# Float64 conversion through a PSUM bank, the last tile's values product in column halves, and another order of the start

## The chip, the cores and the metric

The kernel runs on one core of a Trainium2 chip. The metric is the device time of one execution in microseconds (us), lower is better; it was timed three times, and a further execution was recorded by the hardware profiler.

## The reference

Inputs are q, k and v of 4 batches, 8 heads, 576 positions and 64 columns in float32, and weights in float64: `w_in` 512x2048, `w_out` 2048x512, and for the second MLP `w_gate` and `w_val` 512x1536, `w_out` 1536x512 and a vector `rms_g`. Attention is causal by blocks of 64 positions; its 2304 rows of 512 pass a mish MLP, an RMS norm and a gated MLP:

```python
scores = scale * np.matmul(q, k.transpose(0, 1, 3, 2))
scores = np.where(block_i >= block_j, scores, -1000000000.0)
attn = np.exp(scores - np.max(scores, axis=-1, keepdims=True))
attn = attn / (np.sum(attn, axis=-1, keepdims=True) + 1e-09)
x = np.matmul(attn, v)                      # then (2304, 512)
h = x @ w_in
x = (h * np.tanh(softplus(h))) @ w_out
xn = x / np.sqrt(np.mean(x * x, axis=-1, keepdims=True) + 1e-06) * rms_g
g = xn @ w_gate
out = (g / (1 + np.exp(-g)) * (xn @ w_val)) @ w_out
```

## The kernel before

**Stages.** Attention goes batch by batch, in tiles of 128 queries; 576 queries make four whole tiles and a last one of 64. Such a tile holds scores (`scores`, L986 in f32, L991 and L992 in f16 with the mask), exponentials and their transposes (`probs`), the values product (`av`, L1155 and L1163) and the division by the row sums (`norm_x`, L1195, tile `xfl`). The first MLP has nine tiles of 256 tokens and eight steps of 256 hidden columns in each: the product `h` (L1377 for the first tile, L1386 for the others), the mish function, and the product `y` (L1455 for the first tile, L1447 for the others). The second MLP follows, with `mlp2_o` at its end. Where a product is f16, each factor is split into a high and a low half, and three products are summed (`PASSES`). Scores and values products of batch 0's first tiles, and the whole first MLP tile, are f32.

**The last tile.** Its 64 queries of two heads stand side by side in the 128 columns of one weight tile. The scores go to the two halves of the partitions in matmuls of 64 weight columns (L1009 in f16, L1002 in f32). The values product takes all 128 columns as weights and the 128 value columns of both heads as the moving side (L1163), so half of what it makes is not read: `norm_x` takes the two wanted squares of 64 in two operations.

**Weights.** A float64 chunk (128x512 numbers, 512 KB) is loaded into one of four raw buffers (`load64`, L574, tile `wir` for `w_in`, `wor` for `w_out`, `w2rg`, `w2rv`, `w2ro` for the second MLP in half chunks). Three operations of VectorE build float32 out of the two words of each number (`to_f32`): L586 shifts the high word's mantissa and exponent into place, L594 brings the sign, L614 adds the low word's bits. All three write the destination in SBUF (`wis`, `wos`), the second and third read it again. Column sums (`wiq`, L630), a scale, and the split into f16 halves follow.

**PSUM.** All eight banks are taken: two for `h`, two for `s`, one for `x` (the values product; third bank of `mlp2_o`), two for `y`, and one, `shared`, half of which is `c` (small column sums, L499, L1647; read by VectorE at L501 and L1652), while idle products write into the other half.

**Order.** Each piece of work is recorded by `op(...)` with engine, cost, readers and writers into a `Plan`. A list scheduler (`place`) gives each a planned start from costs and due times, moved by tables (`SHIFT` by part, `FINE` by operation; `PICK` chooses an engine), and the program is emitted in that order. In planned gaps of TensorE in the first 60 us `with_idle` puts idle 128x128 products. The program begins with the queries and all key tiles of batch 0, then the values and `w_in`; attention tiles 0 and 1 come ahead of the first MLP tile, and tile 2 is placed by due time. SyncE issues all loads from one queue, in order.

## Time and profile before

| | us |
|---|---|
| timed runs: lowest, median, highest | 947.88, 949.21, 949.57 |
| profiled execution | 945.24 |
| its span in the trace | 943.5 |
| granted clock of TensorE, mean | 1.00 |

The span is what lies between the first and the last recorded instruction; the profiled execution's own time lies 1.7 us above it, and 4.0 us below the median of the timed runs. TensorE (PE) does the matrix products, VectorE (DVE) the conversions, maxima and normalisations, ScalarE (ACT) the exponentials, GpSimd (POOL) further elementwise work, and SyncE (SP) issues the loads.

### The profile page before, as it was taken

How to read it: one execution, taken by the hardware profiler on the slowest of the kernel's cores; microseconds unless marked ns; L12 is line 12 of the kernel's file. 1: busy time of each engine (PE TensorE's matmuls, PEld its weight loads, DVE VectorE, ACT ScalarE, POOL GpSimd, SP SyncE). 2: the span in 40 equal slices, each digit the busy share in tenths (PEclk: the TensorE clock that was granted, in tenths of full speed). 3: DMA queues.
4: the chain of work that ended last, by engine and by line, in shares of the span. 5: the costliest groups of instructions: out<-in, count | busy, mean ns of one | idle time of the engine just before them, and what ended most of it. 6: DMA issues, size and time to landing. Idle time of an engine off the chain costs nothing. (4 is left out here: it accounts for less than half of the span.)

```text
span 943.5 us, 19993 instructions
## 1 busy us (share of the span) xinstructions
PE 916.3 (97%) x7221; PEld 630.7 (67%) x7221; DVE 816.2 (87%) x1913; ACT 644.4 (68%) x1341; POOL 520.0 (55%) x642
## 2 busy tenths in 40 slices
PE   8999999999999999999999999999999999999997
PEld 7786467476676756667575855767676776767676
DVE  4899989998795868899875999989999999997776
ACT  4669769999797998878674657657666465553431
POOL 1259156484672447557612828589757579573421
PEclk9999999999999999999999999999999999999999
DMA  9864696799757696687863767736295470717011
GB/s 218 215 216 129 195 177 121 130 162 180 152 121 134 111 182 123 141 164 165 171 137 45 125 200 152 140 96 118 79 196 103 121 122 15 140 28 153 6 68 68
DMA packets 317187, 125.44 MB, mean 133 GB/s; under 512 B 296352, under 2 KB 296352, under 8 KB 317088
## 3 DMA queue, kind: packets, MB, share of 16 engines
q1 hardware_dynamic: 317088, 124.17, 62.4%
q8 instruction: 56, 0.92, 0.4%
q14 instruction: 43, 0.35, 0.1%
HBM read 50.07 MB, written 12.98 MB: 67 GB/s over the span
## 5 line engine op out<-in xcount | busy, mean ns | idle before, releaser
L1386 PE MATMUL h<-x,w1i 128*128 128x256 f16 x1536 | 180.5, 273 | 2.1 <-ACT f L1412 1.8
L1447 PE MATMUL y<-w1o,g 128*128 128x512 f16 x768 | 178.9, 379 | 2.0 <-DVE w1o L559 1.6
L1386 PEld LDWEIGHTS <-w1i 128*128 128x128 f16 x1536 | 146.4, 98 | 25.4 <-issue 4.4
L1994 PE MATMUL o<-w2o,pp 128*128 128x256 f16 x1134 | 137.7, 273 | 1.6 <-DVE pp L1904 1.1
L1994 PEld LDWEIGHTS <-pp 128*128 128x128 f16 x1134 | 110.6, 98 | 23.9 <-DVE pp L1904 1.6
L1447 PEld LDWEIGHTS <-g 128*128 128x128 f16 x768 | 71.3, 98 | 80.7 <-issue 4.4
L1835 PEld LDWEIGHTS <-w2g 128*128 128x128 f16 x756 | 73.9, 98 | 47.5 <-issue 2.9
L1835 PEld LDWEIGHTS <-w2v 128*128 128x128 f16 x756 | 73.9, 98 | 46.6 <-issue 2.2
L1051 ACT ACTIVATE e<-s,bias,cS 128x512 f32<-128x512 f32 (+4 forms) x120 | 72.5, 607 | 20.8 <-POOL bias L1035 10.8
L1835 PE MATMUL v_u<-xnT,w2v 128*128 128x384 f16 x432 | 81.6, 326 | 0.3 <-DVE c5v L1916 0.2
L1835 PE MATMUL g_u<-xnT,w2g 128*128 128x384 f16 x432 | 80.1, 326 | 0.4 <-DVE sl11g L1916 0.3
L1026 DVE TENSOR_REDUCE mx<-s 128x1 f32<-128x512 f32 (+4 forms) x128 | 69.9, 556 | 7.1 <-PE s L992 5.9
L1132 POOL TENSOR_TENSOR p<-e,p 128x128 f16<-128x128 f32 (+4 forms) x60 | 56.6, 946 | 33.1 <-ACT p L1128 21.2
L1429 DVE SCALAR_TENSOR_TENSOR g<-f,ich,g 128x512 f16<-128x512 f32 x64 | 54.6, 857 | 10.4 <-ACT g L1424 9.3
L1163 PEld LDWEIGHTS <-pt 128*128 128x128 f16 x1128 | 48.6, 98 | 21.9 <-DMA pt<-p 8.3
L1835 PE MATMUL g<-xnT,w2g 128*128 128x384 f16 x324 | 61.1, 326 | 0.9 <-DVE sl12g L1916 0.6
L1835 PE MATMUL v<-xnT,w2v 128*128 128x384 f16 x324 | 61.5, 326 | 0.5 <-DVE u2v L1916 0.3
L1163 PE MATMUL x<-v,pt 128*128 128x64 f16 (+1 forms) x1128 | 55.0, 199 | 6.4 <-DMA pt<-p 4.9
L1051 ACT ACT_TABLE_LOAD x40 | 51.3, 1283 | 3.5 <-DVE p L1132 2.5
L1412 ACT ACT_TABLE_LOAD x40 | 51.3, 1283 | 2.3 <-PE h L1386 0.9
L1412 ACT ACTIVATE f<-h,ch 128x512 f32<-128x512 f32 x64 | 43.4, 685 | 11.4 <-PE h L1386 6.9
L1035 POOL TENSOR_SCALAR bias<-mx,nS 128x1 f32<-128x1 f32 (+1 forms) x49 | 24.3, 497 | 29.7 <-DVE mx L1026 16.7
(350 smaller groups left out, 2107.9 us busy)
## 6 DMA issues: line engine op xcount, KB each, us to landing
wir<-in_moe_w_in_dram SPq DMA_DIRECT2D x16, 512.0 KB, 5.4
wor<-in_moe_w_out_dram SPq DMA_DIRECT2D x16, 512.0 KB, 4.3
w2rg<-in_moe_w_gate_dram SPq DMA_DIRECT2D x24, 256.0 KB, 3.3
w2rv<-in_moe_w_val_dram SPq DMA_DIRECT2D x24, 256.0 KB, 3.2
w2ro<-in_moe_w_out_dram SPq DMA_DIRECT2D x24, 256.0 KB, 2.9
q<-in_q_dram SPq DMA_DIRECT2D x16, 256.0 KB, 3.7
k<-in_k_dram SPq DMA_DIRECT2D x16, 256.0 KB, 4.2
v<-in_v_dram SPq DMA_DIRECT2D x15, 256.0 KB, 3.8
```

Of the source, the lines that this page charges most:

```text
L1026: lambda z=z, cols=cols: nc.vector.reduce_max(out=mx()[:, cols], in_=ts[z](), axis=AX.X),
L1035: bias_of = lambda eng: eng.tensor_scalar(out=bias()[:, key : keys[-1] + 1 : 2], in0=mx()[:, 2 * key : 2 * keys[-1] + 1 : 4], scalar1=m_op ...
L1051: lambda y=y, z=z, c0=c0, w=w, acc=acc, e=e, h=h: nc.scalar.activation(out=e()[:, c0 : c0 + w], in_=ts[z]()[:, y, :], func=AF.Exp, bias=bi ...
L1132: lo = lambda eng, z=z, ev=ev: eng.tensor_tensor(out=view(p16)[:, z, :, 1, :], in0=ev(0, kt), in1=view(p16)[:, z, :, 0, :], op=ALU.subtract)
L1163: nc.tensor.matmul(xt()[:, cols, :], pv(z)[:, t, ph, :], v16[b, t]()[:, vh, key * w : key * w + w], start=(t == 0 and y == 0), stop=(t == ...
L1386: nc.tensor.matmul(ph()[:, g, :], w1i[fq]()[:, cc, wh, f * P : (f + 1) * P], x()[:, xh * NCC + cc, :], start=(z == 0), stop=(z == 3 * NCC ...
L1412: ACT, t_act(W, 1, True), lambda: nc.scalar.activation(out=e(), in_=phf(), func=AF.Mish, scale=cs()),
L1429: lambda: nc.vector.scalar_tensor_tensor(out=g16()[:, 1], in0=hv(), scalar=sc(), in1=g16()[:, 0], op0=ALU.mult, op1=ALU.subtract),
L1447: nc.tensor.matmul(yps[t, m](), g16()[:, gh, g, m * P : (m + 1) * P], w1o[f]()[:, wh, :], start=(f == 0 and z == 0), stop=(f == NF1 - 1 an ...
L1835: nc.tensor.matmul(b(), w[wo]()[:, wh, cc, :], x()[:, (2 * xo + xh) * 2 + cc, :], start=(first and i == 0), stop=(i == 5), skip_group_chec ...
L1994: nc.tensor.matmul(b()[:, side, :], pps[r][po]()[:, gh, m * P : (m + 1) * P], w[wo]()[:, wh, r, :], start=(first and i == 0), stop=(i == 5 ...
```

## The change

- `to_f32` takes, for `w_in`, `w_out` and the first third of the gate and value weights, a new PSUM bank `v` (tile `cv`): the first two steps write there, the third reads it and writes SBUF. The rest stays as it was.
- The bank `x` is no more: the values product writes the first half of `shared` (columns 0 to 255), `c` stays in 256 to 511, and the idle products write 384 to 511. The freed bank is `v`, which is also the third bank of `mlp2_o`.
- The last tile's values product is two matmuls of 64 weight columns and 64 moving columns, one for each head, instead of one of 128 and 128; `norm_x` is one operation for all tiles.
- Batch 0's f32 keys are loaded and transposed tile by tile (`prep_k32`). Only tiles 0 and 1 of the keys and values come first; the string `START` mixes attention tile 2 and the other loads into the first MLP tile.
- Planner costs, due times and the three tables are others.

```diff
@@ -417,8 +417,13 @@
     def ps_s(shape, name):
         return psum("s", 2, shape, name)
 
-    def ps_x(shape, name):
-        return psum("x", 1, shape, name)
+    def ps_x(name):
+        b = psum("x", 1, [P, NPAIR, D], name)
+        b.whole = lambda: shared()[:, : NPAIR * D].rearrange("p (h d) -> p h d", d=D)
+        return b
+
+    def ps_v(shape, name):
+        return psum("v", 1, shape, name)
 
     def ps_y(i, shape, name):
         return psum(f"y{i}", 1, shape, name)
@@ -574,48 +579,41 @@
-    def to_f32(dst, r, at, pool=False, n=512):
+    def to_f32(dst, r, at, through=True, n=512):
...
+        if through:
+            cnt[0] += 1
+            t, t_one, t_two = ps_v([P, n], f"cv{cnt[0]}"), t_dve(n), t_dve(n)
+        else:
+            t, t_one, t_two = dst, t_dve2(n), t_dvett(n)
         op(
-            DVE, t_dve2(n),
+            DVE, t_one,
             lambda: nc.vector.tensor_scalar(
-                out=dst().bitcast(U32), in0=word(1), scalar1=0x07FFFFFF, scalar2=3,
+                out=t().bitcast(U32), in0=word(1), scalar1=0x07FFFFFF, scalar2=3,
                 op0=ALU.bitwise_and, op1=ALU.logical_shift_left,
             ),
-            r=[r], w=[dst], at=at,
+            r=[r], w=[t], at=at,
         )
         op(
-            DVE, t_dvett(n),
+            DVE, t_two,
             lambda: nc.vector.scalar_tensor_tensor(
-                out=dst().bitcast(U32), in0=word(1), scalar=0xC0000000, in1=dst().bitcast(U32),
+                out=t().bitcast(U32), in0=word(1), scalar=0xC0000000, in1=t().bitcast(U32),
                 op0=ALU.bitwise_and, op1=ALU.bitwise_or,
             ),
-            r=[r], w=[dst], at=at,
+            r=[r], w=[t], at=at,
         )
-        if pool:
-            op(
-                DVE, t_dve2(n),
-                lambda: nc.vector.tensor_single_scalar(word(0), word(0), 29, op=ALU.logical_shift_right),
-                r=[r], w=[(r, 0)], at=at,
-            )
-            op(
-                POOL, t_pool(512),
-                lambda: nc.gpsimd.tensor_tensor(out=dst().bitcast(U32), in0=dst().bitcast(U32), in1=word(0), op=ALU.add),
-                r=[(r, 0), dst], w=[dst], at=at,
-            )
-            return
         op(
-            DVE, t_dvett(n),
+            DVE, t_two,
             lambda: nc.vector.scalar_tensor_tensor(
-                out=dst().bitcast(U32), in0=word(0), scalar=29, in1=dst().bitcast(U32),
+                out=dst().bitcast(U32), in0=word(0), scalar=29, in1=t().bitcast(U32),
                 op0=ALU.logical_shift_right, op1=ALU.bitwise_or,
             ),
-            r=[r], w=[dst], at=at,
+            r=[r, t], w=[dst], at=at,
         )
 
@@ -778,15 +775,15 @@
 
     spares = buf("kv", [P, 4, 512], F32, "spares", "big1", 1)
 
+    def prep_k32(b, tt, at):
+        plan.part = f"k{b}_{tt}"
+        if b not in kT32:
+            kT32[b] = buf("at2" if b % 2 else "kv", [P, NPAIR, S], F32, f"kT32_{b}", f"kT{b % 2}", 1)
+        t = load(k, "k", b, tt, at)
+        transposed(t, f"kT32_{b}_{tt}", kT32[b], tt, at)
+
@@ -1016,10 +1013,10 @@
                 if last:
-                    op(PE, t_mm(w, 2 * passes) + 44, lambda z=z: mm_last(z), r=rd, w=[ts[z]], at=at)
+                    op(PE, t_mm(w, passes) + 60, lambda z=z: mm_last(z), r=rd, w=[ts[z]], at=at)
                 else:
                     for y in range(g):
-                        op(PE, t_mm(n, passes) + 30, lambda y=y: mm_head(y), r=rd + masks, w=[(ts[0], y)], at=at)
+                        op(PE, t_mm(n, passes) + ((100 if n == P else 190) if f32 else 30), lambda y=y: mm_head(y), r=rd + masks, w=[(ts[0], y)], at=at)
                 cols = slice(2 * key + z, 2 * keys[-1] + z + 1, 4)
@@ -1157,20 +1154,22 @@
                             start=(t == 0), stop=(t == kt - 1),
                         )
                     return
-                w = 2 * D if last else D
                 for t in range(kt):
                     for y, (vh, ph) in enumerate(PASSES):
-                        nc.tensor.matmul(
-                            xt()[:, cols, :], pv(z)[:, t, ph, :], v16[b, t]()[:, vh, key * w : key * w + w],
-                            start=(t == 0 and y == 0), stop=(t == kt - 1 and y == 2),
-                        )
+                        for hh in range(2 if last else 1):
+                            sl = slice(BLK * hh, BLK * hh + BLK) if last else slice(0, P)
+                            c0 = (2 * key + hh) * D if last else key * D
+                            nc.tensor.matmul(
+                                xt()[sl, cols, :], pv(z)[:, t, ph, sl], v16[b, t]()[:, vh, c0 : c0 + D],
+                                start=(t == 0 and y == 0), stop=(t == kt - 1 and y == 2),
+                            )
 
...
             op(
-                PE, (56 if last else 34.2) * 3 * kt, mm, r=[pt] + [v16[b, t] for t in range(kt)],
+                PE, 29.2 * 3 * kt + (150 if last else 0), mm, r=[pt] + [v16[b, t] for t in range(kt)],
                 w=[(xt, cols)], at=at,
             )
@@ -1188,16 +1187,13 @@
             xf = buf("at", [P, NPAIR, D], F32, f"xfl{b}_{i}_{half}", "xfl", 1)
-            for hh in range(2 if last else 1):
-                sl, cl = (slice(BLK * hh, BLK * hh + BLK), slice(D * hh, D * hh + D)) if last else (slice(0, P), slice(0, D))
-                op(
-                    DVE, t_dve(256, 1),
-                    lambda sl=sl, cl=cl: nc.vector.tensor_tensor(
-                        out=xf()[sl], in0=xt()[sl, :, cl], in1=r()[sl].unsqueeze(2).to_broadcast([sl.stop - sl.start, NPAIR, D]),
-                        op=ALU.mult,
-                    ),
-                    r=[xt, r], w=[(xf, hh)], at=at,
-                )
+            op(
+                DVE, t_dve(256, 1),
+                lambda: nc.vector.tensor_tensor(
+                    out=xf(), in0=xt(), in1=r().unsqueeze(2).to_broadcast([P, NPAIR, D]), op=ALU.mult,
+                ),
+                r=[xt, r], w=[xf], at=at,
+            )
             t, c0 = divmod(b * NBLK + 2 * i, BPT)
@@ -1317,12 +1313,10 @@
         return T0 + (g / BPT - LEAD) * NS1 * STEP1
 
     prep_q(0, 0, 0.0)
-    prep_k(0, 100.0, KV_PACE)
+    prep_k32(0, 0, 100.0)
+    prep_k32(0, 1, 200.0)
     prep_q(0, 1, 300.0)
-    split_k(0, 5 * KV_PACE, 100.0)
-    prep_v(0, 200.0, KV_PACE)
-    norm_v(0, 7 * KV_PACE)
-    split_v(0, 7 * KV_PACE, 100.0)
+    prep_v(0, 3500.0, 0.0, range(2))
     load_w_in(W_IN_AT, W_IN_PACE)
@@ -1562,15 +1555,28 @@
     firsts = {}
     sums_b = buf("x1", [P, 8 * HK], F32, "sums_b")
 
-    for z in range(2):
-        record_attention(z)
-    queue = [(0, s, mlp1_h(0, s)) for s in range(NS1)]
+    queue, begun = [], 2
+    for c in START:
+        kind, z = c[0], int(c[1])
+        if kind == "a":
+            record_attention(z)
+            begun = max(begun, z + 1)
+        elif kind == "h":
+            queue.append((0, z, mlp1_h(0, z)))
+        elif kind == "k":
+            prep_k32(0, z, K_AT + 1000.0 * z)
+        elif kind == "q":
+            prep_q(0, z, K_AT + 1000.0 * z)
+        elif kind == "v":
+            prep_v(0, V_AT, KV_PACE, range(2, NTT))
+            norm_v(0, VS_AT)
+            split_v(0, VS_AT, 100.0)
     split_w_in(W_SPLIT_AT, W_IN_PACE)
     load_w_out(W_OUT_AT, W_OUT_PACE)
     switch("at2", to_at2, ["rw"], W_OUT_AT)
     for z in queue:
         mlp1_y(*z)
-    order = [(att_time(*TOK[z]), 0, z) for z in range(2, len(TOK))]
+    order = [(att_time(*TOK[z]), 0, z) for z in range(begun, len(TOK))]
     order += [(t_step(n // NS1, n % NS1), 1, n) for n in range(NS1, NT1 * NS1)]
@@ -1631,7 +1637,7 @@
-                    to_f32(plan.part_of(big, cc, slice(c0, c0 + FW // 2)), r, a, n=FW // 2)
+                    to_f32(plan.part_of(big, cc, slice(c0, c0 + FW // 2)), r, a, fq == 0 and nm != "o", FW // 2)
@@ -1982,7 +1988,7 @@
                 chain["o"] += 1
                 z = chain["o"] % 3
                 name = f"o{l}_{chain['o']}"
-                banks.append(ps_y(z, [P, 2, HK], name) if z < 2 else ps_x([P, 2, HK], name))
+                banks.append(ps_y(z, [P, 2, HK], name) if z < 2 else ps_v([P, 2, HK], name))
@@ -2077,7 +2083,7 @@
-    plan.idle = lambda: nc.tensor.matmul(shared()[:, :128], ones_h(), idle_in(), start=True, stop=True)
+    plan.idle = lambda: nc.tensor.matmul(shared()[:, 384:512], ones_h(), idle_in(), start=True, stop=True)
     plan.run()
@@ -2089,206 +2095,213 @@
...
-    "": 780187, "q0_0": -295567, "k0_1": -281404, "k0_2": -105611, "k0_4": -39635, "q0_1": -632121, "v0_0": 4640,
...
-T0, STEP1 = 35000.0, 7376.0
+START = ("a0", "a1", "h0", "h1", "h2", "h3", "h4", "k2", "h5", "q2", "h6", "v0", "a2", "k3", "k4", "h7")
+K_AT, V_AT, VS_AT = 20000.0, 16000.0, 26000.0
+T0, STEP1 = 28000.0, 7376.0
 ATT0, ATT0_PACE = 5000.0, 9000.0
-W_IN_AT, W_IN_PACE = 8000.0, 700.0
-W_OUT_AT, W_OUT_PACE, W_OUT_SPLIT = 60000.0, 2472.0, 1598.0
+W_IN_AT, W_IN_PACE = 3000.0, 1000.0
+W_OUT_AT, W_OUT_PACE, W_OUT_SPLIT = 50000.0, 2472.0, 1598.0
```

SyncE's queue from the program's start, before; `q`, `k`, `v` and `spares` are tiles of batch 0's inputs, `wir` chunks of `w_in`:

```order
L758 DMA q_0_2_88<-in_q_dram 128x8x64
L758 DMA k_1_4_109<-in_k_dram 128x8x64
L758 DMA k_2_5_125<-in_k_dram 128x8x64
L758 DMA k_4_7_127<-in_k_dram 64x8x64
L758 DMA k_0_3_129<-in_k_dram 128x8x64
L758 DMA k_3_6_131<-in_k_dram 128x8x64
L574 DMA wir_0_164<-in_moe_w_in_dram 128x1024
L758 DMA q_1_8_168<-in_q_dram 128x8x64
L758 DMA spares<-in_v_dram 128x8x64
L574 DMA wir_1_192<-in_moe_w_in_dram 128x1024
L574 DMA wir_2_194<-in_moe_w_in_dram 128x1024
L574 DMA wir_3_196<-in_moe_w_in_dram 128x1024
```

and now:

```order
L755 DMA q_0_2_88<-in_q_dram 128x8x64
L755 DMA k_0_3_109<-in_k_dram 128x8x64
L755 DMA v_0_7_125<-in_v_dram 128x8x64
L579 DMA wir_0_127<-in_moe_w_in_dram 128x1024
L579 DMA wir_1_129<-in_moe_w_in_dram 128x1024
L755 DMA k_1_4_131<-in_k_dram 128x8x64
L579 DMA wir_2_164<-in_moe_w_in_dram 128x1024
L755 DMA q_1_5_168<-in_q_dram 128x8x64
L579 DMA wir_3_188<-in_moe_w_in_dram 128x1024
L755 DMA v_2_77_192<-in_v_dram 128x8x64
L755 DMA v_4_81_212<-in_v_dram 64x8x64
L755 DMA v_1_9_221<-in_v_dram 128x8x64
```

Three of the five key tiles went behind the first four chunks of `w_in`.

VectorE ahead of the first product `h`, before; L1195 normalises the second half of attention tile 1, L1026 takes row maxima of tile 2, L586, L594 and L614 convert:

```order
L614 SCALAR_TENSOR_TENSOR wis_0_685<-wir_0_354,wis_0_685 128x512
L586 TENSOR_SCALAR wis_1_730<-wir_1_456 128x512
L1026 TENSOR_REDUCE mx_735<-s_2_0_0_709 128x1
L586 TENSOR_SCALAR wis_2_744<-wir_2_470 128x512
L1026 TENSOR_REDUCE mx_735<-s_2_1_0_725 128x1
L594 SCALAR_TENSOR_TENSOR wis_2_744<-wir_2_470,wis_2_744 128x512
L1187 RECIPROCAL r_766<-r_82_728 128x4
L594 SCALAR_TENSOR_TENSOR wis_1_730<-wir_1_456,wis_1_730 128x512
L614 SCALAR_TENSOR_TENSOR wis_2_744<-wir_2_470,wis_2_744 128x512
L586 TENSOR_SCALAR wis_3_780<-wir_3_505 128x512
L1195 TENSOR_TENSOR xfl_1_1_786<-x_1_81_748,r_766 128x256
L614 SCALAR_TENSOR_TENSOR wis_1_730<-wir_1_456,wis_1_730 128x512
```

and now, where L1192 is that normalisation and `cv` the PSUM tile of the conversion:

```order
L596 TENSOR_SCALAR cv_599<-wir_1_321 128x512
L490 RECIPROCAL p2r_610<-p2d_595 128x1
L493 TENSOR_SCALAR Ev_612<-p2d_595 128x1
L604 SCALAR_TENSOR_TENSOR cv_599<-wir_1_321,cv_599 128x512
L492 TENSOR_SCALAR sv_620<-p2r_610 128x1
L1353 TENSOR_SCALAR ch_624<-E_496,Ev_612 128x1
L612 SCALAR_TENSOR_TENSOR wis_1_628<-wir_1_321,cv_599 128x512
L1192 TENSOR_TENSOR xfl_1_1_634<-shared,r_593 128x256
```

The normalisation stands behind the conversion of the second quarter's second chunk; the steps of its other chunks that ran ahead of it, and the maxima of tile 2, moved behind it.

TensorE at the first group of the last tile's values product, before:

```order
L1002 MATMUL s0_4_2_512_1832<-kT32_0_190,qT_0_4_1364 64x64 x2
L1163 LDWEIGHTS pt_0_4_0_1780
L1163 MATMUL x0_4_162_1838<-v16_0_0_622,pt_0_4_0_1780 128x128
L1163 LDWEIGHTS pt_0_4_0_1780
L1163 MATMUL x0_4_162_1838<-v16_0_0_622,pt_0_4_0_1780 128x128
```

and now:

```order
L1448 MATMUL y0_1_1023<-wos15_1570,g7_1351 128x512
L1162 LDWEIGHTS pt_0_4_0_1708
L1162 MATMUL shared_133<-v16_0_0_626,pt_0_4_0_1708 64x64
L1162 LDWEIGHTS pt_0_4_0_1708
L1162 MATMUL shared_133<-v16_0_0_626,pt_0_4_0_1708 64x64
L1162 LDWEIGHTS pt_0_4_0_1708
L1162 MATMUL shared_133<-v16_0_0_626,pt_0_4_0_1708 64x64
```

Each product became two with half of the weight columns and half of the moving columns, each with its own weight load, in the shared bank.

## Rows read from the trace of the kernel before

**Rows 1.** The page's first part: engine, busy us, share, instructions.
```profile
PE 916.3 (97%) x7221; PEld 630.7 (67%) x7221; DVE 816.2 (87%) x1913; ACT 644.4 (68%) x1341; POOL 520.0 (55%) x642
```

**Rows 2.** By stretch: busy us of each engine, clock, transfer share, GB/s.
```profile
0.00:44.90 44.90, 41.64 (x399) 33.76 (x400) 29.19 (x87) 25.41 (x78) 9.18 (x25) 1.00 0.89 218
44.90:132.90 88.00, 86.43 (x516) 54.84 (x513) 82.33 (x188) 66.55 (x158) 47.21 (x56) 1.00 0.65 174
132.90:500.00 367.10, 352.66 (x3254) 244.99 (x3254) 310.32 (x877) 311.51 (x614) 202.52 (x301) 1.00 0.76 146
500.00:943.50 443.50, 435.56 (x3058) 297.13 (x3056) 394.33 (x765) 240.91 (x494) 261.08 (x260) 1.00 0.49 105
```

**Rows 3.** Groups, PE, 0 to 44.9: busy us, mean ns; idle ahead.
```profile
L2080 PE MATMUL shared<-idle_in,ones_h 128*128 128x128 bf16 x221 | 17.1, 229 | 2.3 <-DVE idle_in L446 2.0 <-DVE p2c L501 0.3
```

**Rows 4.** Time line, 43 to 46: start us, duration us, engine, line, operation.
```profile
43.19 0.91 PE L986 MATMUL s<-kT,qT 64*128 64x384 f32 x2
43.30 0.42 DVE L1195 TENSOR_TENSOR xfl<-x,r 128x256 f32<-128x256 f32 x1 [0.93 <-PE x L1155]
...
44.06 0.34 PE L2080 MATMUL shared<-idle_in,ones_h 128*128 128x128 bf16 x3
...
44.24 0.39 PE L1209 MATMUL xt<-ident,xfl 128*128 128x128 f32 x2
...
44.91 1.30 PE L1377 MATMUL h<-x,wis 128*128 128x256 f32 x5
```

**Rows 5.** SyncE's time line; then landing times of `wir`, 20 to 40.
```profile
26.17 2.56 SPq L574 DMA_DIRECT2D wir<-in_moe_w_in_dram  x4
...
DMA to landing us min/median/max: 3.9/5.7/7.3
```

**Rows 6.** Conversions: groups 60 to 125, then lines' ns min/median/max, first and last start.
```profile
L614 DVE SCALAR_TENSOR_TENSOR wos<-wor,wos 128x512 uint32<-128x512 uint32 x16 | 13.9, 866 | 0.0
L594 DVE SCALAR_TENSOR_TENSOR wos<-wor,wos 128x512 uint32<-128x512 uint32 x16 | 12.6, 794 | 0.0
L586 DVE TENSOR_SCALAR wos<-wor 128x512 uint32<-128x512 uint32 x16 | 7.5, 468 | 0.6 <-DMA wor<-in_moe_w_out_dram 0.5
...
L586 DVE TENSOR_SCALAR wis<-wir x16: 407/417/1372, 12.6 to 63.9; 128x512 uint32<-128x512 uint32 x16
...
L594 DVE SCALAR_TENSOR_TENSOR wos<-wor,wos x16: 668/682/1647, 68.8 to 112.8; 128x512 uint32<-128x512 uint32 x16
```

**Rows 7.** VectorE reading PSUM: a maximum of the time line; line L2015.
```profile
28.10 0.69 DVE L1026 TENSOR_REDUCE mx<-s 128x2 f32<-128x512 f32 x1 [0.18 <-PE s L992]
...
L2015 DVE SCALAR_TENSOR_TENSOR acc<-o,co,acc x26: 467/734/752, 604.7 to 861.1; 128x512 f32<-128x512 f32 x14, 128x256 f32<-128x256 f32 x12
```

**Rows 8.** TensorE's time line, 130 to 134 and 489 to 493.
```profile
131.73 1.01 PE L1163 MATMUL x<-v,pt 128*128 128x128 f16 x15
132.89 1.36 PE L1386 MATMUL h<-x,w1i 128*128 128x256 f16 x11
...
489.44 1.58 PE L1386 MATMUL h<-x,w1i 128*128 128x256 f16 x13
490.95 0.41 PE L1009 MATMUL s<-kT,qT 128*64 128x512 f16 x2
...
491.41 0.20 PE L1009 MATMUL s<-kT,qT 128*64 128x64 f16 x2
491.44 0.20 PE L1009 MATMUL s<-kT,qS 128*64 128x64 f16 x2
491.57 1.49 PE L1386 MATMUL h<-x,w1i 128*128 128x256 f16 x12
492.89 0.28 PE L1163 MATMUL x<-v,pt 128*128 128x128 f16 x2
```

**Rows 9.** The shared bank, time line: columns 256 on written, and read.
```profile
573.54 0.27 PE L1647 MATMUL shared<-junk,ones_h 128*128 128x256 bf16 x1
...
589.02 0.41 DVE L1652 TENSOR_REDUCE w2m<-shared 128x1 f32<-128x256 f32 x1
```

38 lines of the change are left out of this document (14 added, 24 removed), and 365 rows, old and new, of tables (FINE, PICK, SHIFT).

## The prediction

> **What bounds the kernel now.** I began with the shares of the engines. TensorE is busy in 97% of the span, VectorE in 87% [rows 1], so the matrix unit sets the end almost everywhere, and work taken off another engine pays only where TensorE waits for it. The table by stage shows where that is. The granted clock is 1.00 in all four stretches [rows 2], so no stretch can be won by a faster clock. Up to 44.90 us, where the first MLP product starts, TensorE counts 41.64 us busy, but 17.1 of them are 221 idle products, put in where the plan has a gap [rows 3]; on top 44.90 - 41.64 = 3.3 us are free. So some 20 us of the start are waiting. From 44.90 to 132.90 TensorE is free for 1.6 us, from 132.90 to 500 for 14.4 us, after 500 for 7.9 us of 443.50 [rows 2]. (Busy counts overlapping latencies, so the real slack is somewhat larger.) The start is where a change of order can pay most; later on, only fewer or shorter TensorE instructions pay.
>
> What does the start wait for? The detailed time line shows it: the last half of the attention tile is normalised on VectorE at 43.30, transposed at 44.24, and the first MLP product starts at 44.91, with idle products in between [rows 4]. The queue of transfers shows the other end: the loads of the second quarter of `w_in` are issued from 26.17 on, and a weight chunk takes 5.7 us to land in the median [rows 5]; all bytes go at 218 GB/s with the transfer engines 0.89 busy [rows 2]. The start is thus a stream of bytes, a stream of conversions on VectorE behind it, and attention mixed into both.
>
> **The change part by part.**
>
> *The start.* Counted from the order of the transfers: up to and with the first chunk of the second quarter 6400 KB stand in the queue before, 5248 KB now. At 218 GB/s that is 30.1 us against 24.7 us; before, the chunk landed at 26.17 + 5.7 = 31.9, so 1.8 us lie ahead of the stream, and now it lands near 26.5. On VectorE the normalisation that releases the first MLP product now stands behind the next chunk's conversion, which has 6016 KB up to it (28.3 + 1.8 = 30.1 us). Three operations of 0.69 us [rows 7] follow, then the normalisation, and from its start to the first MLP product it took 44.91 - 43.30 = 1.6 us [rows 4]: the product can start at 30.1 + 2.1 + 1.6 = 33.8 at the earliest. The other end goes by VectorE: its first conversion ran at 12.6 [rows 6]; the first chunk now has 640 KB fewer ahead, 3.0 us. Ahead of that normalisation VectorE now has less to do: three steps of 0.42 and three of 0.68 fewer, a half-height split pair (some 2.1) and two row maxima (1.1) fewer, one copy more (0.5), and six first steps that cost 0.27 more each (1.6): 4.3 us in all. So it comes at 43.3 - 3.0 - 4.3 = 36.0 and the product at 37.6. I take 35.5, near the middle: VectorE worked only 29.19 us of the 44.90 [rows 2], so it wasn't packed, but it is not idle enough to follow the bytes. But four score heads and 16 transposes that stood ahead of the first MLP product now stand behind it. A head took from 43.19 to 44.06, 0.87 us, of which the rows show the 0.91 of its product; two transposes took 0.39 [rows 4], of which one is latency, so about 0.1 each: 4 x 0.87 + 16 x 0.1 = 5.1 us which must be done later. Gain: 44.9 - 35.5 - 5.1 = **4.3 us**, bounds 44.9 - 33.8 - 5.1 = 6.0 and 44.9 - 37.6 - 5.1 = 2.2.
>
> *The conversion through PSUM.* Before, the three steps of a chunk took 468 + 794 + 866 = 2.13 us in the mean. The row of the second step shows 682 in the median and up to 1647: some are stretched to more than double while another engine is at work [rows 6]. Operations that read PSUM here run at 0.69 us for 128x512 [rows 7], and the fused one with a PSUM operand never exceeds 752 in 26 instances [rows 7]. So a chunk takes 3 x 0.69 = 2.07, 0.06 less; for 32 chunks that is 2 us of VectorE. An unstretched chunk took 0.42 + 0.68 + 0.68 = 1.78, and the early ones get 0.29 dearer, which is in the 4.3 above. On the path I count 0: after the start VectorE is covered by TensorE's work, and if that cover is gone the price is between -2 us and 32 x 0.29 = +9 us. A single bank holds each chunk until its third step, but the three steps follow one another on VectorE anyway.
>
> The Trainium skill ("VectorE: DVE Perf Modes", Why PSUM operands drop a tier) says that an fp32 operation with a PSUM operand runs at the slowest tier; that speaks against this part, and the rows agree for the read (0.69 against 0.42). Were a step that only writes PSUM to keep 0.42, 32 x 0.27 = 8.6 us of VectorE more would be saved.
>
> *The last tile of each batch.* 240 products of 128x128 become 480 of 64 columns. Fifteen of the old ones took 1.01 us and two 0.28 [rows 8]: 13 more cost 0.73, so each is 0.056 us apart. The new form, 128 rows by 64 weight columns with 64 moving, stands already in the last tile's scores: two halves start at 491.41 and 491.44, 0.03 apart [rows 8], so a pair costs about 0.028 beyond the first. 240 x (0.056 - 0.028) = 6.7 us less. Against it stands going into and out of such a stretch. Eleven MLP products took 1.36 and thirteen 1.58 [rows 8], 0.11 each; thirteen from 489.44 on would let the next start at 490.87, and it starts at 490.95. On the way out, the last half starts near 491.47 and the next MLP product at 491.57. Together 0.1 + 0.1 = 0.2 us. The order has 35 stretches of 64-column products against 21: 14 x 0.2 = 2.8 us. Net **3.9 us** gained; bounds 6.7 gained (switches hidden) and, if halves run one after another at 0.056 for the pair, 2.8 lost. Normalisation there is one VectorE operation instead of two; covered, 0.
>
> *The shared bank.* The values product, the column sums `c` and the idle products now share one bank, tracked as a whole where they touch. In eight places in the order a values product waits for VectorE's read of `c`. Behind the waiting product TensorE's whole queue is held, so VectorE's lateness falls on the path. The read normally has one operation ahead at worst, 0.69 [rows 7]: 8 x 0.69 = 5.5 at most, 0 at least; I take **0.5**, near 0, since the order goes by planned starts that contain this wait. The dangerous ones are the column maxima of the second MLP's weights: one was written at 573.54 and read at 589.02 [rows 9].
>
> *The rest* (re-searched order, planner costs) has no price in a row; 0, with up to a third of the 14.4 + 7.9 us of later slack [rows 2] as a bound to the good and the same to the bad.
>
> Sum: -4.3 - 3.9 + 0.5 + 0 = -7.7 us. The profiled execution took 945.24, 4.0 us below the median of the timed ones, 949.21; it would take 937.5, and the median is 949.2 - 7.7 = **941.5 us**.
>
> **The rivals.**
>
> *The weight stream holds the start.* The bytes up to the last chunk of `w_in` are nearly the same (12928 KB before, 12544 now, 1.8 us), and the same VectorE converts them. If the first MLP product runs early only to wait for later quarters, the gain of 4.3 is given back. Against it: VectorE's first conversion moves up too. Then -3.9 + 0.5 = -3.4: 945.8 us.
>
> *The halves don't overlap*, or switches eat them: -4.3 + 2.8 + 0.5 = -1.0, 948.2 us. Against it are the two starts 0.03 apart [rows 8]; for it, that there only four stand in a row, and here 30 and more with a new weight load for each. The Trainium skill ("TensorEngine Tiling (Array Packing)", Gotcha 2: Feature Incompatibilities, and Key Properties) states that column tiling excludes the fast weight load and that a change of the tiling mode drains TensorE. By the first the halves would be bound by their weight loads; the rows show a pair at no such price, and the gap of 0.2 us round the stretch bears out the second.
>
> *A wait in the shared bank takes the place of the gain (slower).* Three values products of batch 3 wait for reads of column maxima. If VectorE reads one as late as in [rows 9], 589.02 - 573.54 = 15.5 us, with some 13 left of it when the product comes up, TensorE stands still: -4.3 - 3.9 + 13 = +4.8, 954 us. It turns the sign from about 8 us of waiting on. Against it: the order puts the read ahead of the normalisation that this product needs.
>
> *The middle shrinks as well*: a third of the later slack, 22.3 / 3 = 7.4, on top: -15.1, 934 us.
>
> **How the numbers follow.** Forecast 0.57 (937 to 945.5), weight stream 0.15, halves 0.10, shared bank 0.08, middle 0.10. A measurement of this kernel tells 0.2%, 1.9 us, from no change. Faster by more: 0.57 + 0.15 + 0.10 = 0.82; same 0.10; slower 0.08. The range reaches down to the middle's case and up to that of the halves: 932 to 948.5, leaving out the shared bank and the ends.
>
> **What would show it.** The first MLP product should start at 34 to 37.6 us, a weight chunk's three VectorE steps at 0.69 each with no stretched ones, pairs of last-tile products 0.03 us apart, with 0.2 us round each stretch, and no gap over 0.7 us ahead of a values product. Wrong would be: a first product early and then gaps ahead of the next quarters; halves 0.056 apart; one gap of many us ahead of a values product late in the attention of the last batch; or a gain that lies after 133 us.

## The result

The changed kernel took 938.56 us in the median (936.99 to 939.51), the kernel before 948.55 over the same runs: a ratio of 0.9895 with a 95% interval of 0.9872 to 0.9917. A second set of runs gave 0.9877 (0.9860 to 0.9893). The forecast, 941.5 us with a range of 932 to 948.5, held in sign and size. Most of its terms did not.

The profiled execution of the changed kernel took 936.99 us with a span of 935.2, 8.3 less than before (943.5), and its mean granted clock was 1.00 as well. The page's head, to be held against [rows 1]:

```profile
span 935.2 us, 20362 instructions
PE 911.7 (97%) x7395; PEld 622.2 (67%) x7396; DVE 804.6 (86%) x1920; ACT 643.0 (69%) x1330; POOL 508.3 (54%) x644
```

The table by stage, cut where the first MLP product, the first f16 product and the last attention end now (the columns are those of [rows 2]):

```profile
0.00:38.05 38.05, 33.76 (x305) 28.04 (x306) 26.25 (x79) 20.73 (x65) 5.25 (x22) 1.00 0.85 219
38.05:131.90 93.85, 93.70 (x558) 57.55 (x558) 88.25 (x208) 73.25 (x168) 42.71 (x64) 1.00 0.68 183
131.90:492.00 360.10, 348.55 (x3408) 238.68 (x3407) 301.49 (x876) 305.85 (x605) 214.39 (x309) 1.00 0.77 147
492.00:935.20 443.20, 435.73 (x3128) 297.89 (x3125) 388.63 (x759) 243.18 (x494) 245.96 (x251) 1.00 0.49 106
```

The start got 6.9 us shorter (38.05 against 44.90), but the stretch behind it got 5.9 us longer (93.85 against 88.00): the first f16 product comes at 131.9 instead of 132.9. So of the 8.3 us only 1.0 lie ahead of that point, and another profiled execution of the same kernel (`same_again`) had these two products at 37.4 and 132.6. The stretch up to the end of attention holds the rest: 360.1 us against 367.1 (with ends a few us apart in the program, since the order differs), with TensorE free for 11.6 us instead of 14.4.

The first product and what stands ahead of it, to be held against [rows 4]:

```profile
34.92 1.10 PE L1152 MATMUL shared<-v,pt 128*128 128x64 f32 x8 [0.21 <-ACT pt L1080]
34.92 0.68 DVE L612 SCALAR_TENSOR_TENSOR wis<-wir,cv 128x512 uint32<-128x512 uint32 x1
...
36.06 0.42 DVE L1192 TENSOR_TENSOR xfl<-shared,r 128x256 f32<-128x256 f32 x1 [0.46 <-PE shared L1152]
...
36.54 0.83 PE L2086 MATMUL shared<-idle_in,ones_h 128*128 128x128 bf16 x12 [0.51 <-DVE xfl L1192]
37.20 0.39 PE L1205 MATMUL xt<-ident,xfl 128*128 128x128 f32 x2
...
38.06 0.70 PE L1370 MATMUL h<-x,wis 128*128 128x256 f32 x2
```

The normalisation at 36.06 waited 0.46 us for the values product and that one for the transposed exponentials. The conversion of the weights was through at 35.60. The attention chain came last, not the weights.

The conversion's steps, and the half products, to be held against [rows 6] and [rows 8] (the first three rows: ns min/median/max; the last: start, duration, count):

```profile
L596 DVE TENSOR_SCALAR cv<-wor x16: 677/684/696, 65.4 to 110.2; 128x512 uint32<-128x512 uint32 x16
L604 DVE SCALAR_TENSOR_TENSOR cv<-wor,cv x16: 675/685/696, 66.2 to 111.4; 128x512 uint32<-128x512 uint32 x16
L612 DVE SCALAR_TENSOR_TENSOR wos<-wor,cv x16: 670/677/693, 67.3 to 112.8; 128x512 uint32<-128x512 uint32 x16
...
130.34 0.66 PE L1162 MATMUL shared<-v,pt 128*64 128x64 f16 x30
```

No step through PSUM is stretched any more: the longest in these rows is 696 ns (720 for `w_in`), where 1647 stood. Thirty halves take 0.66 us; without some 0.2 of latency that is 0.016 each, 0.032 a pair, as forecast.

### The profile page after: what moved, and what is told of

Its sections match the earlier page's. It is cut to its first block, busy times and chain, and to the rows that moved or that the text cites. A ratio compares the mean times of both kernels' runs of the same rounds, so it can differ in the third digit from the quotient of the medians.

```text
span 935.2 us, 20362 instructions
## 1 busy us (share of the span) xinstructions
PE 911.7 (97%) x7395; PEld 622.2 (67%) x7396; DVE 804.6 (86%) x1920; ACT 643.0 (69%) x1330; POOL 508.3 (54%) x644
## 4 chain that ended last, share of the span: by engine, by line
PE 41%; DVE 11%; ACT 5%; POOL 3%; DMA 2%; issue 2%; SPq 0%; DVEq 0%; ACTq 0%; POOLq 0%
PE o L2000 10%; PE y L1440 6%; PE g_u L1841 6%; PE v_u L1841 5%; PE h L1379 4%; PE g L1841 4%; PE v L1841 4%; DMA pt<-p 1%; PE shared L1162 1%; DVE g L1422 1%; DVE mx L1023 1%; ACT e L1048 1%; DVE pp L1910 1%; DVE w2o L564 0%; PE s L988 0%
## 5 line engine op out<-in xcount | busy, mean ns | idle before, releaser
L1379 PEld LDWEIGHTS <-w1i 128*128 128x128 f16 x1536 | 145.7, 98 | 25.2 <-issue 3.9
L2000 PE MATMUL o<-w2o,pp 128*128 128x256 f16 x1134 | 138.0, 272 | 1.0 <-POOL pp L1910 0.6
L1129 POOL TENSOR_TENSOR p<-e,p 128x384 f16<-128x384 f32 (+4 forms) x60 | 58.6, 977 | 36.4 <-ACT p L1125 19.7
L1422 DVE SCALAR_TENSOR_TENSOR g<-f,ich,g 128x512 f16<-128x512 f32 x64 | 56.7, 886 | 17.1 <-ACT g L1417 10.8
L1162 PEld LDWEIGHTS <-pt 128*128 128x128 f16 (+1 forms) x1368 | 44.5, 103 | 26.6 <-issue 10.7
L1162 PE MATMUL shared<-v,pt 128*128 128x64 f16 (+1 forms) x1368 | 50.5, 195 | 5.5 <-DMA pt<-p 2.6
L530 POOL TENSOR_SCALAR p<-e 128x128 f16<-128x128 f32 (+2 forms) x55 | 29.2, 534 | 27.5 <-ACT e L1048 21.1
```

Source lines behind the costliest of these rows:

```text
L530: nc.gpsimd.tensor_scalar(out=out_, in0=in_, scalar1=by, scalar2=1.0, op0=ALU.mult, op1=ALU.mult)
L1129: lo = lambda eng, z=z, ev=ev: eng.tensor_tensor(out=view(p16)[:, z, :, 1, :], in0=ev(0, kt), in1=view(p16)[:, z, :, 0, :], op=ALU.subtract)
L1162: nc.tensor.matmul(xt()[sl, cols, :], pv(z)[:, t, ph, sl], v16[b, t]()[:, vh, c0 : c0 + D], start=(t == 0 and y == 0), stop=(t == kt - 1 a ...
L1379: nc.tensor.matmul(ph()[:, g, :], w1i[fq]()[:, cc, wh, f * P : (f + 1) * P], x()[:, xh * NCC + cc, :], start=(z == 0), stop=(z == 3 * NCC ...
L1422: lambda: nc.vector.scalar_tensor_tensor(out=g16()[:, 1], in0=hv(), scalar=sc(), in1=g16()[:, 0], op0=ALU.mult, op1=ALU.subtract),
L2000: nc.tensor.matmul(b()[:, side, :], pps[r][po]()[:, gh, m * P : (m + 1) * P], w[wo]()[:, wh, r, :], start=(first and i == 0), stop=(i == 5 ...
```

## The experiments

All but one of the variants keep the instruction order of the kernel they start from, apart from what is named; so what changes first is the edited operations. That one is `after_replan`. `after` in a label is the changed kernel. Times are medians, ratios go to the kernel before on the same chip (950.5, 950.8 and 950.1 us in the three groups of runs). The changed kernel was timed again in the first group only; beside the others its 938.5 us stand for it, so a difference of a microsecond across groups says little.

### The last tile's halves

**The changed kernel again.**

> The changed kernel once more, as the reference for the runs beside it: 938.5 us, 0.9895 of the kernel before. Nothing is told apart by it alone.

938.53 us, 0.9877 (0.9860 to 0.9893).

**Halves alone in the kernel before.**

```diff
-                        nc.tensor.matmul(
-                            xt()[:, cols, :], pv(z)[:, t, ph, :], v16[b, t]()[:, vh, key * w : key * w + w],
...
+                        for hh in range(2 if last else 1):
...
+                            nc.tensor.matmul(
+                                xt()[sl, cols, cl], pv(z)[:, t, ph, sl], v16[b, t]()[:, vh, c0 : c0 + D],
...
```

> The kernel before, its whole order kept, with the one edit that the last tile's values product goes in two halves of 64 weight and 64 moving columns. The forecast's theory: pairs 0.03 us apart save 6.7 us, 15 more stretches with 0.2 us round each cost 3.0, so 3.7 us faster, a ratio of 0.996. Rival 1, the switches are hidden or free: 6.7 us faster, 0.993. Rival 2, the halves don't overlap: 3 us slower, 1.003.

950.09 us, 0.9996 (0.9978 to 1.0013): nothing of the 3.7 us. Two waits grew in its profile, and behind each the granted clock stood near 0.50, the lower of its levels (1.2 instead of 2.4 GHz). By stretch (columns as in [rows 2]):

```profile
116.00:119.00 3.00, 3.00 (x31) 2.42 (x30) 2.26 (x10) 2.12 (x5) 0.00 (x0) 0.50 0.47 87
...
408.00:412.50 4.50, 2.31 (x23) 1.19 (x21) 3.39 (x13) 3.15 (x9) 2.25 (x5) 1.00 1.04 122
412.50:416.00 3.50, 3.29 (x25) 2.39 (x26) 1.88 (x6) 0.81 (x3) 3.03 (x7) 0.53 1.23 215
```

TensorE worked 2.31 of 4.50 us up to 412.5, and then ran 3.5 us at 0.53. In the kernel before the same two stretches read 1.00. The mean clock of its twelve runs was 0.993 to 0.998, 0.996 on average, against 0.998 for the kernel before beside them. That is up to 0.0025 x 944 = 2.4 us more lost than there, if TensorE was busy in all of the span, so the drops can have eaten most of the gain; that they did is inferred, not shown.

**All 128 weight columns in the changed kernel.**

```diff
-                                xt()[sl, cols, :], pv(z)[:, t, ph, sl], v16[b, t]()[:, vh, c0 : c0 + D],
-                                start=(t == 0 and y == 0), stop=(t == kt - 1 and y == 2),
+                                xt()[:, cols, :], pv(z)[:, t, ph, :], v16[b, t]()[:, vh, c0 : c0 + D],
+                                start=(t == 0 and y == 0 and hh == 0), stop=(t == kt - 1 and y == 2 and hh == (1 if last else 0)),
```

> The changed kernel, its order kept; each of the last tile's 480 half products takes all 128 weight columns (64 moving), so no half runs beside another and no stretch changes the array's division. It sums the two heads' products, which is wrong data at the right volume. The forecast's theory: 480 products 0.029 us apart instead of 240 pairs 0.028 apart cost 6.7 us more, and 15 stretches of 0.2 us fall away, 3.7 us slower than the changed kernel. Switches free: 6.7 slower. Halves that don't overlap: 3 us faster.

940.14 us, 0.9899 (0.9882 to 0.9916): 1.6 us over the changed kernel's median, where 3.7 were expected; the intervals overlap, and neither nothing nor 3.7 is excluded. TensorE's rows are sharper. One group with the MLP products on either side, in the changed kernel and then here:

```profile
134.93 1.48 PE L1379 MATMUL h<-x,w1i 128*128 128x256 f16 x12
136.34 0.66 PE L1162 MATMUL shared<-v,pt 128*64 128x64 f16 x30
136.94 4.11 PE L1379 MATMUL h<-x,w1i 128*128 128x256 f16 x36
```

```profile
135.34 1.48 PE L1379 MATMUL h<-x,w1i 128*128 128x256 f16 x12
136.66 1.04 PE L1162 MATMUL shared<-v,pt 128*128 128x64 f16 x30
137.54 4.09 PE L1379 MATMUL h<-x,w1i 128*128 128x256 f16 x36
```

The group itself is 0.38 us longer here, 6.1 for all 16 groups. So the pairs do run beside one another. But from the start of the one MLP group to that of the next it is 2.01 us with halves and 2.20 here: with the switches on either side only 0.19 us a group are left, 3.0 in all.

**One head, 128 weight columns.**

```diff
-                        for hh in range(2 if last else 1):
-                            sl = slice(BLK * hh, BLK * hh + BLK) if last else slice(0, P)
+                        for hh in range(1):
+                            sl = slice(0, P)
```

> The changed kernel with only the first head of each pair in the last tile's values product, all 128 weight columns and 64 moving: 240 products, none of them a half; the second head's product is left out. Same pure product time as the halves, no change of the array's division round it. The forecast's theory: the 15 stretches' 0.2 us fall away, 3.0 us faster than the changed kernel. If the switches are free or hidden: no difference.

936.13 us, 0.9849 (0.9833 to 0.9865): 2.4 us below the changed kernel, 3.0 expected. It spends about as much on the products (15 in 0.60 us) and switches the array's division nowhere round them. The price of some 0.2 us for each stretch stands. Between this and `after_wide` lie 240 products of 0.029 us, 7.0 us; the medians differ by 4.0, and the scatter of their nine executions leaves 2.5 to 6.5 (95%). So some of TensorE's work cost no time; the likeliest reason, not shown, is that something else ends last round these products. The halves' net gain is thus 1.6 us by the medians and 3.0 by TensorE's rows in the changed kernel, not clear of noise, and none is seen in the kernel before.

### The conversion, the shared bank and the start

**Conversion in SBUF, order kept.**

```diff
-                out=t().bitcast(U32), in0=word(1), scalar1=0x07FFFFFF, scalar2=3,
+                out=dst().bitcast(U32), in0=word(1), scalar1=0x07FFFFFF, scalar2=3,
...
-                out=t().bitcast(U32), in0=word(1), scalar=0xC0000000, in1=t().bitcast(U32),
+                out=dst().bitcast(U32), in0=word(1), scalar=0xC0000000, in1=dst().bitcast(U32),
...
-                out=dst().bitcast(U32), in0=word(0), scalar=29, in1=t().bitcast(U32),
+                out=dst().bitcast(U32), in0=word(0), scalar=29, in1=dst().bitcast(U32),
```

> The changed kernel, its order kept; the first two conversion steps write the SBUF destination, as the kernel before did, and the PSUM bank v stays unused by them. The forecast's theory, VectorE is covered: 938.5 us, no change, a chunk's three steps back at some 1.8 us unstretched and over 2.1 in the mean. Rival, the stretched steps were on the path: 2 to 5 us slower than the changed kernel. Rival, PSUM makes early chunks dearer and these are on the path: 1 to 2 us faster.

951.43 us, 1.0008 (0.9992 to 1.0024): 12.9 us slower than the changed kernel, the whole gain, and far beyond both rivals of the expectation. The forecast had priced this part at nothing. The first MLP product is no later (37.2 against 38.1 and 37.4), but the first f16 product comes at 138.0 instead of 131.9. One stretch between, of the changed kernel and then of this one:

```profile
45.00:90.00 45.00, 44.86 (x247) 30.33 (x246) 44.12 (x101) 37.59 (x79) 24.08 (x32) 1.00 0.68 208
```

```profile
45.00:90.00 45.00, 39.40 (x197) 25.91 (x196) 44.31 (x85) 34.44 (x70) 32.08 (x29) 1.00 0.62 180
```

VectorE is busy for 44 of 45 us in both, but in these 44 us it gets through 101 instructions in one and 85 in the other. GpSimd needs 32.08 us for 29 instructions instead of 24.08 for 32. TensorE falls to 39.40. Its waits between 45 and 100 us, here (in the changed kernel that view has no row):

```profile
PE wiq L628 <- POOL junk L624: 2.1, 2, 1.7
PE h L1370 <- DVE wis L612: 1.2, 1, 1.2
PE tpp L1094 <- DVE pt L1105: 0.9, 1, 0.9
```

So both converting engines are late. The reason is in their groups. VectorE's second and third step here, ns min/median/max:

```profile
L604 DVE SCALAR_TENSOR_TENSOR wos<-wor,wos x16: 656/686/1442, 70.2 to 119.6; 128x512 uint32<-128x512 uint32 x16
L612 DVE SCALAR_TENSOR_TENSOR wos<-wor,wos x16: 654/683/1564, 72.0 to 120.8; 128x512 uint32<-128x512 uint32 x16
```

And GpSimd's groups between 45 and 115 us, of this kernel and then of the changed one (busy us, mean ns):

```profile
L551 POOL TENSOR_TENSOR w1i<-wis,w1i 128x512 f16<-128x512 f32 x14 | 19.6, 1414 | 0.3
L530 POOL TENSOR_SCALAR wis<-wis,s 128x512 f32<-128x512 f32 x12 | 14.4, 1215 | 8.6 <-PE h L1370 7.6 <-DVE s L492 0.9
L1032 POOL TENSOR_SCALAR bias<-mx 128x1 f32<-128x1 f32 x13 | 5.8, 447 | 17.2 <-DVE mx L1023 16.6
```

```profile
L551 POOL TENSOR_TENSOR w1i<-wis,w1i 128x512 f16<-128x512 f32 x16 | 18.4, 1163 | 3.4 <-ACT w1i L545 3.0
L530 POOL TENSOR_SCALAR wis<-wis,s 128x512 f32<-128x512 f32 x12 | 8.5, 726 | 8.1 <-PE h L1370 8.0
L1032 POOL TENSOR_SCALAR bias<-mx 128x1 f32<-128x1 f32 x14 | 2.7, 192 | 20.0 <-DVE mx L1023 19.5
```

The same GpSimd operation takes 1215 ns beside SBUF conversions and 726 beside PSUM ones; the tiny bias, on which the exponentials wait, 447 against 192. GpSimd's own instructions were not edited, so in these rows the two engines hold each other up when both work on SBUF. The Trainium skill ("SBUF — State Buffer", SBUF: two separate sides) describes it: VectorE and GpSimd share one pair of ports as an exclusive lock, which VectorE takes for an operation in a two-port mode or, against a GpSimd operation that reads SBUF, with two SBUF inputs, and the loser waits for the whole instruction. The rows on both sides fit that.

The kernel before pays the same prices and does not lose by them. The same stretch there, and two GpSimd groups between 45 and 115 us:

```profile
45.00:90.00 45.00, 44.87 (x247) 33.45 (x246) 43.62 (x88) 35.20 (x71) 30.24 (x29) 1.00 0.56 174
```

```profile
L525 POOL TENSOR_SCALAR wis<-wis,s 128x512 f32<-128x512 f32 x6 | 6.9, 1155 | 4.4 <-PE h L1377 2.5 <-DVE s L487 1.8
L1035 POOL TENSOR_SCALAR bias<-mx 128x1 f32<-128x1 f32 x11 | 5.0, 455 | 15.7 <-DVE mx L1026 15.3
```

TensorE is busy for 44.87 us beside operations that are as slow. Its order covers them; the changed order does not.

The stretch up to the first f16 product holds 6.1 of the 15.1 us between the two profiled spans. The other 9 lie between that product and the end of attention (the changed kernel, then `after_direct`):

```profile
131.90:500.90 369.00, 357.44 (x3542) 244.30 (x3541) 305.72 (x884) 311.54 (x613) 215.31 (x310) 1.00 0.76 147
```

```profile
138.00:516.30 378.30, 360.59 (x3542) 244.37 (x3541) 312.80 (x885) 312.50 (x613) 216.37 (x310) 1.00 0.77 143
```

TensorE is free for 17.7 us there instead of 11.6. What it waits for in that part was not followed to its cause.

**The values product in a bank of its own,** on top of the last one.

```diff
-        b.whole = lambda: shared()[:, : NPAIR * D].rearrange("p (h d) -> p h d", d=D)
         return b
...
-        return psum("v", 1, shape, name)
+        b = psum("v", 1, shape, name)
+        b.tag = "x_0"
+        return b
```

> As after_direct, and the values product in the bank that the conversion left free, so that it shares its bank with neither the column sums nor the idle products. The forecast's theory: the shared bank costs 0.5 us, so 938 us against after_direct. Rival: the idle products' waits for the normalisation and the waits for the column sums lie on the path, 2 to 3 us faster than after_direct, with the first MLP product 0.5 us or more earlier.

949.94 us, 0.9989 (0.9974 to 1.0005), 1.5 us below `after_direct` (0.6 to 2.5 by the twelve times of each). The first MLP product comes at 36.1 instead of 37.2; 0.6 of that lies behind the last values product, where twelve idle products no longer wait 0.51 us for the normalisation. The price of sharing is 1.5 us by the medians, in the bounds of 0 to 5.5, above the 0.5 taken.

**Half the bytes.**

```diff
-        op(DMA, t_rows(P, 4 * n), lambda: nc.sync.dma_start(out=r().bitcast(U32), in_=src.bitcast(U32)), w=[r], at=at)
+        m = n if pool == "kv" else n // 2
+        op(DMA, t_rows(P, 4 * n), lambda: nc.sync.dma_start(out=r()[:, :m].bitcast(U32), in_=src[:, : src.shape[1] * m // n].bitcast(U32)), w=[r], at=at)
...
+            half = r()[:, :n].bitcast(U32).rearrange("p (c w) -> p c w", w=2)[:, :, i]
+            return half.unsqueeze(1).to_broadcast([P, 2, n // 2])
...
```

> The changed kernel, its order kept; of each chunk of w_in and w_out only half of the bytes are loaded and used twice, so the weights are wrong and 8 MB less move. If the stream of bytes sets the start (first chunk of the second quarter near 26.5 us in the forecast), that chunk lands some 4 us earlier, the first MLP product starts up to 2 us earlier than at 38.1, and the kernel is 1 to 3 us faster. If the attention chain or VectorE sets it, the first MLP product stays within 0.5 us and the time within 1 us.

937.81 us, 0.9863 (0.9838 to 0.9889); the first MLP product at 37.4.

**The second conversion step on one column.**

```diff
+        w = 1 if n == 512 else n
...
-                out=t().bitcast(U32), in0=word(1), scalar=0xC0000000, in1=t().bitcast(U32),
+                out=t()[:, :w].bitcast(U32), in0=word(1)[:, :w], scalar=0xC0000000, in1=t()[:, :w].bitcast(U32),
```

> The changed kernel, its order kept; the second conversion step of the chunks of w_in and w_out works on one column instead of 512, so their signs are left out and VectorE has 32 x 0.6 = 19 us less to do, most of it before 115 us. If VectorE sets the start or the first MLP tile, the first MLP product comes 1 to 3 us earlier and the kernel is 2 to 5 us faster. If TensorE or the attention chain sets it, the time stays within 1 us.

937.44 us, 0.9859 (0.9834 to 0.9885); the first MLP product at 37.0. (It came at 38.1 and 37.4 in two profiled executions of the changed kernel, so these shifts are hardly clear of that.) Neither 8 MB nor 17 us of VectorE (32 steps of 0.69 us that now take 0.16) move the time by more than about 1 us. In the changed kernel the start is held neither by the bytes nor by VectorE, but by attention and then by TensorE, which is busy for 93.70 of the 93.85 us that follow.

### Does the conversion pay in another order?

**The operations of the changed kernel in the order of the kernel before.** In that order VectorE mixes the steps of several chunks, which one bank can't hold; so each chunk's first two steps were moved directly ahead of its third, in the chunks that go through PSUM.

```diff
...
+        t = Buf(lambda: ps, [P, n], F32, f"cv{len(plan.ops)}", "x_0", 1) if through else dst
...
+        if through:
+            three = plan.ops[-3:]
+            plan.held |= {three[0].idx, three[1].idx}
+            plan.joined[three[2].idx] = three[:2]
...
```

> The kernel before in its own order of loads, products and attention, with the changed kernel's operations: conversion through a PSUM bank (w_in, w_out, first third of gate and value), values product in the shared bank, last tile in halves; each chunk's first two steps stand directly ahead of its third, since one bank holds one chunk. Theory after the earlier runs: the conversion is worth 10 us or more by itself, 938 to 941 us. Rival: it pays only in the order that was searched for it, and here the time stays at 946 to 951 us.

964.8 us, 1.0164 (1.0136 to 1.0192).

**The same, with the steps in SBUF.**

```diff
-        t = Buf(lambda: ps, [P, n], F32, f"cv{len(plan.ops)}", "x_0", 1) if through else dst
+        t = dst
```

> As before_psum, but the two first steps write the SBUF destination as in the kernel before: what remains is the grouping of the steps, the shared bank and the halves. Theory: 948 to 953 us, no gain, so that the difference to before_psum is the conversion's. Rival: if grouping alone frees VectorE, 940 to 945 us.

965.24 us, 1.0151 (1.0124 to 1.0178). Both expectations were missed: moving the steps, with the shared bank and the halves, costs some 15 us, and beside that PSUM or SBUF makes no difference that can be measured. (The halves alone cost nothing in `before_halves`; the bank alone was not tried in this order, but idle products wait 3.0 and 2.2 us in the two for the normalisation that reads it.) Part of it is the clock: its mean was 0.991 and 0.994 in the executions of the two, 0.998 in the kernel before, up to 6 and 4 us by the same estimate as for `before_halves`. The first f16 product comes at 145.6 and 145.7. The waits of TensorE in `before_psum`, its longest (us, times, longest):

```profile
PE shared L1175 <- DMA pt<-p: 6.4, 5, 2.4
PE s L1000 <- ACT e L1060: 4.5, 10, 0.9
PE s L995 <- ACT e L1060: 3.9, 1, 3.9
```

The time line shows what stands ahead of the exponential of the 3.9 us:

```profile
118.02 0.68 DVE L1035 TENSOR_REDUCE mx<-s 128x1 f32<-128x512 f32 x1
...
118.79 0.19 POOL L1044 TENSOR_SCALAR bias<-mx 128x1 f32<-128x1 f32 x1 [7.47 <-DVE mx L1035]
...
120.85 0.63 ACT L779 ACTIVATE junk<-wos 128x512 bf16<-128x512 f32 x1 [1.93 <-DVE wos L619]
...
121.48 0.67 ACT L1060 ACTIVATE e<-s,bias 128x512 f32<-128x512 f32 x1
...
122.29 1.26 PE L995 MATMUL s<-kT,qT 64*128 64x512 f32 x2 [3.86 <-ACT e L1060]
```

Its bias was ready at 118.98. But ahead of it on ScalarE stands a pass over converted weights, which waited 1.93 us for the third step of its chunk. The maximum itself stood behind three steps of the chunk before. So in this order the place of the grouped steps in the queues is late, and at this wait, the only one followed, cheaper steps could have saved only a part.

**SBUF conversion, planned anew with the changed kernel's tables.**

```diff
     def to_f32(dst, r, at, through=True, n=512):
+        through = False
```

> The changed kernel with all conversions in SBUF, and the planner told so (its costs, and no PSUM bank between the steps), its tables kept: it may order the work anew. Theory, the stretched operations themselves cost: 947 to 953 us, like after_direct. Rival, after_direct lost only because its order was planned for other durations: 938 to 944 us.

962.74 us, 1.0126 (1.0100 to 1.0152), slower even than `after_direct`. The likeliest reason, not shown, is that the tables fit one set of costs; planned with others they lose what had been searched for. The mean clock of its executions was 0.994, too. The run can't tell what an order searched for SBUF conversions and the new start would give. That stays open, and with it how much of the 12.9 us is the conversion's own price and how much the misfit of durations to an order made for others.

### Closing the longest wait

In `same_again` the table by stretch round 155 us shows a wait and what follows:

```profile
154.50:156.00 1.50, 0.13 (x2) 0.00 (x0) 1.50 (x4) 1.41 (x2) 1.18 (x2) 1.00 1.19 238
156.00:159.50 3.50, 2.93 (x21) 2.23 (x22) 3.45 (x11) 3.02 (x6) 2.37 (x4) 0.51 0.66 142
159.50:163.00 3.50, 3.50 (x27) 2.23 (x25) 3.50 (x8) 3.49 (x9) 1.99 (x5) 1.00 0.38 65
```

and the time line the instruction that waited:

```profile
156.57 0.64 PE L1162 MATMUL shared<-v,pt 128*128 128x64 f16 x9 [1.94 <-DVE xfl L1192]
```

A values product waits for the normalisation that reads the bank, which stands behind other work of VectorE. The edit moves that normalisation and its factor up (787 and 788 are their numbers, 724 that of the scale they need):

```diff
-        for o in sorted(self.ops, key=lambda o: (o.start, o.idx)):
+        row = sorted(self.ops, key=lambda o: (o.start, o.idx))
+        early = [o for o in row if o.idx in (787, 788)]
+        row = [o for o in row if o.idx not in (787, 788)]
+        z = 1 + next(i for i, o in enumerate(row) if o.idx == 724)
+        for o in row[:z] + early + row[z:]:
```

> The changed kernel with two VectorE operations moved up by four places: the last normalisation of batch 0 and its factor, directly behind the scale that they need. A values product waited 1.94 us for that normalisation at 154.6 us, and in most executions the granted clock stood at half for some 3.4 us behind it. Theory: the wait shrinks to about 0.5 us and the clock stays, 2 to 3 us faster than the changed kernel. Rival: what was late there is late at the next wait, within 1 us.

936.73 us, 0.9859 (0.9834 to 0.9884): the fastest median of a kernel that computes everything, 1.8 us below the changed kernel's, but the intervals overlap. Its time line shows why it isn't more:

```profile
153.35 0.22 PE L1166 MATMUL shared<-v,pt 128*128 128x64 f16 x2 [0.58 <-DVE xfl L1196]
154.14 0.36 PE L1166 MATMUL shared<-v,pt 128*128 128x64 f16 x7 [0.58 <-DVE v L568]
```

The wait for the bank shrank to 0.58, but the split of the values, pushed back by the move, now holds the same product for another 0.58. The granted clock is 0.81 from 153 to 156 and 0.62 from 156 to 159. The shorter waits did not keep it up here.

## Right and wrong, step by step

The sum of the forecast was -4.3 - 3.9 + 0.5 + 0 = -7.7 us. The medians moved by 10.0, the profiled spans by 8.3. The terms:

- **The start, -4.3.** Its form was right, its size was not. The first MLP product came at 38.1 and, in `same_again`, at 37.4, beyond and at the late end of the bounds of 33.8 to 37.6. I had let the byte stream or VectorE end last, and neither does: with half the bytes it comes at 37.4, with 17 us less VectorE work at 37.0. Attention's own chain, which I had left out of the bounds, comes last. With the 5.1 us of work put behind it, the gain is 44.9 - 38.1 - 5.1 = 1.7 (2.4 in `same_again`), and 1.0 (0.3) is left at the first f16 product. The rival of a stream that gives the gain back was right in its effect (945.8 would have left the start nothing) and wrong in its cause.
- **The conversion, 0.** This is the step that failed: "after the start VectorE is covered by TensorE's work". [rows 2] was a warning: 82.33 busy us of 88.00 between 44.9 and 132.9 leave VectorE little room. But the cover held in the kernel before, where TensorE was free for 1.6 us of that stretch beside stretched steps. I carried it over to another order without a reason, and there it did not hold: with SBUF steps TensorE is free for 5.6 of the 45 us from 45 to 90. I had also priced VectorE's steps alone, while the rows of GpSimd show that the other engine pays as much: 6 us for one group of twelve instructions (14.4 against 8.5). Undone in the changed order, the part costs 12.9 us, and even my bound to the good side was 2. My bound to the bad side, +9 us for PSUM's dearer unstretched steps, did not show; a chunk's steps were 0.27 dearer, and that was hidden.
- **The last tile, -3.9.** The pair's spacing (0.032 against 0.028) and the price of a switch (2.4 us for all against 2.8) were nearly right; with both, TensorE's rows leave 3.0 of the 3.9. The rest of the miss is that not all of TensorE's saved work came out as time: 240 products of 0.029 us changed the median by 4.0, not 7.0. Net 1.6 us by the median of `after_wide`, not clear of noise, and nothing in the kernel before. The exclusion of the fast weight load that the forecast took from the Trainium skill ("TensorEngine Tiling (Array Packing)", Gotcha 2: Feature Incompatibilities) shows no price as a rival: thirty halves, each with its own load, took 0.66 us. The drain at a change of the mode (Key Properties) agrees with the 0.1 us that the halves start later behind an MLP group than the whole products do.
- **The shared bank, +0.5.** About 1.5 by `after_ownbank`. No wait for column maxima of many us appeared, so the slower rival did not come true. The mark "no gap over 0.7 us ahead of a values product" was missed by the 1.94 us, which came from the bank's other reader, the normalisation.
- **The rest, 0.** `before_psum`, which has the operations and, but for the moved steps, the other order, is 26 us slower than the changed kernel, and `after_replan` 24. As far as these runs go, the order and the durations belong together; neither has a price of its own.

So the number came out by luck: two terms were too large, by 1.9 to 4.0 and by 0.9 to 2.3 us, and one that I had set to zero carries the gain in this order. One of the forecast's own signs of being wrong, a gain that lies after 133 us, came true: 7.3 of the 8.3 us lie there, where only part of the last tile's 3.9 was to come. The prices found by undoing one part at a time (1.0, 1.6 and 12.9 gained, 1.5 lost) make 14.0 us and not 10.0, so they do not stand by themselves either. What is shown is that without the PSUM conversion the changed order loses everything; that the conversion alone brings the gain is not, since in the order of the kernel before it brought nothing.
